# Turning one pair of token tiles on VectorE and through DRAM instead of on TensorE, in a two-layer Fourier mixer with MLPs

## The chip, the cores and the metric

One core of one Trainium2 chip runs the whole program. The metric is the device time of one execution in microseconds (us); the median over the runs is compared. On the core five engines run their own queues in order: TensorE (in the profile PE for matmuls, PEld for weight loads), VectorE (DVE), ScalarE (ACT), GpSimd (POOL) and SyncE (SP), which here issues most DMAs. An engine waits on semaphores for the others, so an instruction that waits holds up all that stands behind it in its queue.

## The reference

`x` is 2048 tokens by 576 features. Two layers each do a Fourier step and an MLP step, both with a layer norm ahead and a residual:

```python
def _A_ref(x, dft_seq_re, dft_seq_im, dft_hid_re, dft_hid_im):
    a = jnp.einsum("bsd,ed->bse", x, dft_hid_re)
    b = jnp.einsum("bsd,ed->bse", x, dft_hid_im)
    return jnp.einsum("ts,bse->bte", dft_seq_re, a) - jnp.einsum("ts,bse->bte", dft_seq_im, b)
def _B_ref(x, w1, b1, w2, b2):
    y = _layernorm(x, axis=-1)
    h = _gelu(jnp.einsum("bsd,df->bsf", y, w1) + b1)
    return jnp.einsum("bsf,fd->bsd", h, w2) + b2
...
    x = x + _A_ref(_layernorm(x, axis=-1), ...)
    x = x + _B_ref(_layernorm(x, axis=-1), ...)
    x = x + _A_ref(_layernorm(x, axis=-1), ...)
    x = x + _B_ref(_layernorm(x, axis=-1), ...)
```

`w1` is 576 by 4608, `w2` is 4608 by 576. All is 32-bit floating point.

## The kernel before, in words

**Arithmetic.** Every large product is done in three TensorE passes over a high and a low part of each operand (`PASSES`): ScalarE copies the high part into a rounded 32-bit type, VectorE (or GpSimd) subtracts it from the value for the low part. Most products also use a scheme with seven block products for a two by two block matrix: sums of blocks are formed first, and the seven results are added up by VectorE, GpSimd and ScalarE.

**Order of the program.** A layer begins with a sequence phase (`Sequence`), which multiplies by the 2048 by 2048 matrices `cs` and writes `uv_mid`. Then, for each half of the tokens, a feature phase (`hidden`) multiplies by the 576-wide matrices, adds the residual and normalizes, and an MLP (`mlp`) follows. So there are two sequence phases, four feature phases and four MLPs. The MLP of a half is a generator that is already advanced while the feature phase ends.

**Sequence phase** (`Sequence.run`). After the first two token blocks it goes through steps, seven per output tile `t` (products in `ORDER`), each 24 matmuls of 128x288 (`mms`). In step `n` the queues get, in this order: loads of `cs` blocks that have found a free place (`load_c`); the low part of step `n + 2` (`low`, VectorE, with up to one more subtraction that forms a sum of blocks in place and then frees a block); once per tile `sums` for the next tile, one addition and one subtraction of 128x1024 on VectorE; the high part of step `n + 3` (`high`, ScalarE); the matmuls; and `post`, which adds the product up. At the end of a tile `turned` transposes it in 32x32 squares on VectorE.

**Pumps.** A generator `weights` prepares the seven block sums of `w1` in the background, one piece in two pumps: high part on ScalarE, low part on VectorE, a sum for a later piece on GpSimd, and a store to `w1_parts`. The store is issued by ScalarE during the first sequence phase, by SyncE later. The sequence phase pumps twice at the end of most steps. In the first MLP the pumps stand at fixed places of a group (`BEHIND`), and the blocks of `w2` are prepared there too (`make`, with `due` places). By the second half all weights come ready from DRAM.

**Feature phase** (`hidden`, half = 8 tiles of 128 tokens, `n` = 0 to 7). Step `n` loads tile `n + 2`, splits the turned input of tile `n + 1` (`turn`: ScalarE high, VectorE low), finishes the norm of tile `n - 1` (ScalarE), and does 54 matmuls (`KH` = 9 parts, 3 passes, 2 halves of features). Then VectorE adds the product to the residual and takes the statistics (`norms`, `stats`; GpSimd does the power). Line 198 is the helper for additions, 201 for subtractions, 211 for all large matmuls, 208 for VectorE's 32x32 transposes, 258 for normalizing.

The MLP needs the normalized tokens with features on partitions. Tiles are turned in pairs: pair `j` is tiles `2j` and `2j + 1` of the order, which give four blocks b12, b22, b11 and b21 (feature half by token half). The three first pairs go like this: `rests` spreads the last 32 features of each block (96 columns, ScalarE), `turn_blocks` transposes on TensorE (eight of 128x128, line 991; four of 128x96, line 994) into PSUM, ScalarE copies out (995, 996), `turn_sums` makes high and low parts of three blocks in two groups and then four sums with VectorE, and `turn_parts` makes the high and low parts of the sums. `turn_blocks` of pairs 0, 1 and 2 stands after the product of `n` = 2, 4 and 6, and `turn_sums` of pairs 0 and 1 inside `n` = 3 and 5.

The last pair goes another way, since nothing is left to hide it: the last tile is normalized by VectorE (line 962), VectorE forms the sums first (t1, t3, t2, t4 in this order; t2 needs t1, t4 needs t2), and `turn_y` transposes all seven blocks on TensorE (14 transposes, line 1035; 7 of the rests, line 1045) in four groups of two blocks, groups in the order `(2, 4, 0, 6)` of the list `blocks`. Each group's high part is copied by ScalarE and its low part subtracted by VectorE (`split`). Matmuls of the MLP for the first half of the tokens (`next(mlp)`) fill TensorE before and between. After them the MLP's products 1, 6, 2, 5, 7, 3, 4 for the second half begin, product `i` with the block at place `RIGHT_T[i]` of `y`.

Of the kernel before, what the change touches and what calls it, by code (L numbers as in the profile page):

```python
# [15 lines left out]
P = 128  # L16
# [26 lines left out]
RIGHT_T = {3: 0, 2: 1, 1: 2, 5: 3, 7: 4, 6: 5, 4: 6}  # L43
# [21 lines left out]
BEHIND = (0, 2, 2, 4, 5, 6, 15, 16, 16, 17, 17, 19, 21, 21)  # L65
H_AT = (8704, 22400)
# [94 lines left out]
def spectral_mixer(ctx: ExitStack, tc: tile.TileContext, x, dh, c0, cs, w1, b1, w2, b2, out):  # L161
# [16 lines left out]
    w1s = nc.dram_tensor("w1_parts", (NQ, 7, P, 5 * P), F32, kind="Internal").ap()  # L178
    w2s = nc.dram_tensor("w2_parts", (NG, 7, P, 2, 2 * DH), F32, kind="Internal").ap()
# [84 lines left out]
    def weights():  # L264
# [44 lines left out]
        high(0)  # L309
        for n in range(7 * NQ):  # L310
            yield
            low(n)
            if n + 1 < 7 * NQ:
                high(n + 1)
            yield
            keep(n)
# [13 lines left out]
    class Sequence:  # L330
# [357 lines left out]
        def sums(self, t):  # L688
            add(nc.vector, self.tmp(NP, P), self.block(t, 2), self.block(t, 3))
            sub(nc.vector, self.block(t, 2), self.block(t, 2), self.block(t, 0))  # L690
# [67 lines left out]
        def run(self, hidden):  # L758
# [12 lines left out]
            for n, (t, i) in enumerate(steps):  # L771
# [3 lines left out]
                if n % 7 == 2 and t + 1 < NT:  # L775
                    self.sums(t + 1)
                self.load_c()
                if n + 3 < len(steps):
                    self.high(*steps[n + 3])
# [13 lines left out]
                if n % 7 != 2 and n > 3 and (t < NT - 1 or n % 7 < 4):  # L793
                    pump()
                    pump()
# [133 lines left out]
    def hidden(h, mlp):  # L929
# [16 lines left out]
        t8 = {}  # L946

        def norms(n):
# [9 lines left out]
            if n < NP - 1:  # L958
                shift(mv)
                normalize(z, tile_x, mv)  # L960
# [11 lines left out]
            yield  # L972

# [10 lines left out]
        def turn_blocks(j):  # L984
# [4 lines left out]
            for n, e in enumerate((2, 0, 1, 3)):  # L989
# [3 lines left out]
            for n, e in enumerate((2, 0, 1, 3)):  # L993
                nc.tensor.transpose(b[:96, 0, n * P:(n + 1) * P], es(7, 96)[:, e], ident)  # L994
# [14 lines left out]
        def turn_sums(j):  # L1009
            x = t8[j](8 * DH)[:, 6 * P:].rearrange("p (b k) -> p b k", b=4)  # L1010
            b11, b12, b22, b21 = (x[:, k] for k in range(4))
            parts(j, slice(2, 4), slice(0, 2))
            parts(j, slice(0, 1), slice(2, 3))
# [10 lines left out]
        def turn_y(j):  # L1024
            v = t8[j](8, DH)
            at = slice(j * P, (j + 1) * P)
            blocks = (1, 3, 2, 4, 5, 6, 7)
# [23 lines left out]
        for n in range(NP):  # L1051
# [6 lines left out]
            if n >= 2 and n % 2 == 0:  # L1058
                rests(n // 2 - 1)
            if n == NP - 3:  # L1060
# [25 lines left out]
            if n in (3, 5):  # L1086
                turn_parts((n - 3) // 2)
            if n >= 2 and n % 2 == 0:
# [32 lines left out]
    def mlp(hid, store, first, ends, before, after):  # L1121
# [3 lines left out]
        stores[0] = nc.sync  # L1125
# [383 lines left out]
```

## Time and profile before

| | |
|---|---|
| median of 3 runs | 2622.78 us (2622.07 to 2624.11) |
| the profiled execution | 2624.75 us |
| its span, first to last instruction | 2623.0 us |
| granted TensorE clock | 1.000 |
| busy: PE, PEld, DVE, ACT, POOL | 2614.4, 2466.3, 1836.8, 1120.2, 791.5 us |
| first sequence phase, its steps | about 79 to 372 us |
| first feature phase and MLP | to about 848 us |
| moved by DMA | 544.91 MB, 208 GB/s over the span |

A group in the profile is a line of the kernel, an engine, an operation and the tiles that it writes and reads, with its count, its busy time, the mean of one in ns, and the idle time of that engine just before, with what ended it. `R` and `A` are the two large areas in SBUF (rounded and plain type), `bank` is PSUM. A wait is put down to the instruction that released it last. The chain is followed back from the last instruction; a piece on it is what the end hung on.

### The profile page before, as it was taken

What the parts mean: (1) busy time and instruction counts of PE and PEld (TensorE: products, weight loads), DVE (VectorE), ACT (ScalarE), POOL (GpSimd) and SP (SyncE); (2) the same over time, 40 slices, a digit from 0 to 9 for tenths busy, and PEclk for the clock granted to TensorE, in tenths of its full rate; (3) what the DMA queues carried; (4) which work ended last, traced back from release to release, by engine and by line L of the source; (5) the groups of instructions that cost most, each with busy time, mean ns of one, the idle gap of its engine ahead of it and who ended that gap; (6) DMA issues with size and microseconds to landing.
All of it is one profiled execution on the core that took longest, in us unless ns stands there. A gap on an engine that the chain in (4) does not pass through costs nothing.

```text
span 2623.0 us, 44794 instructions
## 1 busy us (share of the span) xinstructions
PE 2614.4 (100%) x17252; PEld 2466.3 (94%) x17252; DVE 1836.8 (70%) x2580; ACT 1120.2 (43%) x1821; POOL 791.5 (30%) x638
## 2 busy tenths in 40 slices
PE   9999999999999999999999999999999999999999
PEld 9999999899999989998999999999999999899998
DVE  8999987778787765556687776576555557655555
ACT  7555555555553443333354333353333325433332
POOL 5334333544444332222251000132122233322222
PEclk9999999999999999999999999999999999999999
DMA  6667676778788666676544343756666685666664
GB/s 226 223 236 234 234 255 215 266 278 301 279 299 300 178 202 195 194 222 210 173 175 135 122 124 124 211 159 194 193 195 194 195 268 169 199 195 195 194 194 155
DMA packets 223238, 544.91 MB, mean 208 GB/s; under 512 B 23712, under 2 KB 74912, under 8 KB 222880
## 3 DMA queue, kind: packets, MB, share of 16 engines
q1 hardware_dynamic: 210496, 513.91, 62.2%
q10 hardware_dynamic: 12528, 28.12, 2.8%
q8 instruction: 137, 2.24, 0.3%
q14 instruction: 77, 0.63, 0.1%
HBM read 429.87 MB, written 114.72 MB: 208 GB/s over the span
## 4 chain that ended last, share of the span: by engine, by line
PE 92%; DVE 5%; DMA 1%; issue 1%; POOL 1%; ACT 0%; DVEq 0%; ACTq 0%; SPq 0%; POOLq 0%
PE bank L211 91%; DVE R L201 3%; DVE A L201 1%; DMA w_parts<-R 1%; DMA A<-in_cs 0%; PE bank L991 0%; DVE A L198 0%; PE bank L1035 0%; DVE moments L242 0%; PE bank L994 0%; ACT R L698 0%; DMA A<-in_w 0%; DMA R<-w_parts 0%; PE bank L1045 0%; POOL A L198 0%
## 5 line engine op out<-in xcount | busy, mean ns | idle before, releaser
L211 PE MATMUL bank<-R 128*128 128x288 f32 (+2 forms) x16972 | 2585.9, 314 | 3.9 <-DVE R L201 1.2
L211 PEld LDWEIGHTS bank<-R 128*128 128x128 f32 x16972 | 2434.8, 189 | 150.8 <-DVE R L201 4.3
L198 DVE TENSOR_TENSOR A<-bank,A 128x576 f32<-128x576 f32 (+3 forms) x812 | 567.6, 707 | 510.2 <-PE bank L211 457.7
L201 POOL TENSOR_TENSOR R<-A,R 128x512 fp32r<-128x512 f32 (+1 forms) x292 | 380.0, 1310 | 912.4 <-ACT R L1299 560.6
L201 DVE TENSOR_TENSOR R<-A,R 128x1024 fp32r<-128x1024 f32 (+10 forms) x534 | 535.0, 1028 | 34.6 <-ACT R L698 14.3
L1299 ACT ACTIVATE R<-A 128x512 fp32r<-128x512 f32 x288 | 177.5, 630 | 356.4 <-DVE A L201 219.5
L198 POOL TENSOR_TENSOR A<-A 128x576 f32<-128x576 f32 (+2 forms) x102 | 155.0, 1527 | 531.1 <-ACT A L743 338.9
L1234 ACT ACTIVATE bank<-bank,b1t 128x512 f32<-128x512 f32 (+1 forms) x224 | 144.9, 647 | 350.5 <-DVE bank L198 233.6
L698 ACT ACTIVATE R<-A 128x1024 fp32r<-128x1024 f32 x196 | 205.6, 1054 | 123.8 <-PE bank L211 61.0
L198 DVE TENSOR_TENSOR bank<-bank,A 128x512 f32<-128x512 f32 (+1 forms) x228 | 152.3, 670 | 147.7 <-PE bank L211 147.0
L201 POOL TENSOR_TENSOR A<-A 128x288 f32<-128x288 f32 (+3 forms) x152 | 190.3, 1255 | 198.1 <-DVE R L201 103.6
L201 DVE TENSOR_TENSOR A<-A 128x1024 f32<-128x1024 f32 (+3 forms) x166 | 163.5, 989 | 6.2
L201 DVE TENSOR_TENSOR R<-bank,R 128x512 fp32r<-128x512 f32 x232 | 156.1, 676 | 5.5 <-ACT R L1299 5.0
L1299 ACT ACTIVATE R<-bank 128x512 fp32r<-128x512 f32 x216 | 121.0, 595 | 33.9 <-PE bank L211 33.9
L201 DVE TENSOR_TENSOR A<-bank,A 128x512 f32<-128x512 f32 x144 | 98.1, 681 | 0.4
L1261 ACT ACTIVATE A<-bank 128x512 f32<-128x512 f32 (+1 forms) x76 | 43.7, 575 | 120.2 <-PE bank L211 120.1
L284 ACT ACTIVATE R<-A 128x256 fp32r<-128x256 f32 x126 | 51.9, 412 | 63.7 <-DMA w_parts<-R 27.1
L1234 ACT ACTIVATE A<-bank,b1t 128x512 f32<-128x512 f32 (+1 forms) x76 | 50.5, 665 | 63.4 <-DVE bank L198 63.4
L232 POOL TENSOR_TENSOR moments<-moments,power 128x1 f32<-128x1 f32 x32 | 25.5, 797 | 134.9 <-DVE moments L234 117.5
L285 ACT ACTIVATE R<-A,power,middle 128x128 fp32r<-128x128 f32 x126 | 60.6, 481 | 0.0
L258 ACT ACTIVATE A<-A,moments 128x576 f32<-128x576 f32 x58 | 49.3, 867 | 23.7 <-DMA A<-x_mid 11.7
L198 DVE TENSOR_TENSOR A<-A 128x1024 f32<-128x1024 f32 x28 | 35.8, 1277 | 20.0 <-DMA A<-in_cs 12.3
(70 smaller groups left out, 612.9 us busy)
## 6 DMA issues: line engine op xcount, KB each, us to landing
R<-w_parts SPq DMA_DIRECT2D x504, 320.0 KB, 3.4
R<-w_parts SPq DMA_DIRECT2D x189, 576.0 KB, 3.7
A<-in_cs SPq DMA_DIRECT2D x112, 512.0 KB, 4.5
w_parts<-R SPq DMA_DIRECT2D x63, 576.0 KB, 6.2
w_parts<-R ACTq DMA_DIRECT2D x75, 320.0 KB, 4.3
w_parts<-R SPq DMA_DIRECT2D x51, 320.0 KB, 4.9
uv_mid<-A SPq DMA_DIRECT2D x28, 576.0 KB, 5.4
A<-in_w SPq DMA_DIRECT2D x72, 192.0 KB, 5.4
```

The lines of the kernel that those rows point to most:

```text
L198: engine.tensor_tensor(dst, a, b, op=op)
L201: engine.tensor_tensor(dst, a, b, op=OP.subtract)
L211: nc.tensor.matmul(o, a, b, start=start, stop=stop, skip_group_check=True)
L232: nc.gpsimd.tensor_tensor(mv[:, 3:4], mv[:, 2:3], power[:, 0:1], op=OP.pow)
L258: nc.scalar.activation(dst, src, AF.Identity, bias=mv[:, 4:5], scale=mv[:, 3:4])
L284: nc.scalar.activation(t[:, 1:4:2], src[:, 0:3:2], AF.Copy)
L285: nc.scalar.activation(t[:, 2], src[:, 1], AF.Identity, bias=power[:, 2:3], scale=middle)
L698: nc.scalar.activation(self.cells[t, i](2, NP, P)[:, 0], self.source(t, i), AF.Copy)
L1234: nc.scalar.activation(dst, src, AF.Gelu_apprx_tanh, bias=bias(f))
L1261: nc.scalar.activation(up, o, AF.Copy)
L1299: nc.scalar.activation(H[q, k](2, TC)[:, 0], src, AF.Copy)
```

## The change

Several things are changed at once.

1. In the three feature phases after the first (`flip`, true where the matrices come ready), pair 0 is no longer turned on TensorE. ScalarE normalizes its two tiles into squares of 32 features (`mixed`); VectorE transposes the first tile's two blocks 32 by 32 (`turn_early`, in `n` = 1); in `n` = 2 it forms the four sums and transposes five blocks (`turn_late`). The squares are written to a DRAM tensor `y_mid` (`write_first`, SyncE, three DMAs for each of two parts) and read back in the order that the MLP needs (`read_first`, four DMAs each). `first_parts` then makes the high parts (three ScalarE copies) and low parts (three VectorE subtractions), in `n` = 3 for the first two blocks and in `n` = 4 for the other five, ahead of that tile's addition. `rests`, `turn_blocks`, `turn_sums` and `turn_parts` of pair 0 are gone there.
2. The seven blocks of `y` get another order, in all four phases (`RIGHT_T`, `turn_blocks`, `turn_sums`, `turn_y`), so that the two blocks and the five lie side by side. `turn_sums` makes the parts of its three blocks in one group. In `turn_y` the order of groups stays `(2, 4, 0, 6)`, with another list of blocks.
3. In the sequence phase `sums` is done in two pieces, the addition at place 3 of a tile and the subtraction at place 4, not both at 2. Of the two pumps of a step one goes ahead of `high` of step `n + 3`; the step without pumps is the last of a tile. In `weights` the store of a piece comes one pump later, with the next high part.
4. In the first MLP's group 0 three more steps of `make(0)` are done, and group 1 has two pumps fewer (`BEHIND_1`).

The diff, cut to its core:

```diff
-RIGHT_T = {3: 0, 2: 1, 1: 2, 5: 3, 7: 4, 6: 5, 4: 6}
+RIGHT_T = {2: 0, 1: 1, 3: 2, 4: 3, 5: 4, 6: 5, 7: 6}
+FIRST_AT = ((4224, 0), (10464, 11232))
+BEHIND_1 = (0, 2, 2, 4, 15, 16, 16, 17, 17, 19, 21, 21)
...
-        high(0)
+        done = 0
         for n in range(7 * NQ):
+            if n:
+                keep(n - 1)
+            if done == n:
+                high(n)
+                done += 1
             yield
             low(n)
-            if n + 1 < 7 * NQ:
+            if len(stores) > 1 and n + 1 < 7 * NQ:
                 high(n + 1)
+                done += 1
             yield
-            keep(n)
+        keep(7 * NQ - 1)
...
-                if n % 7 == 2 and t + 1 < NT:
-                    self.sums(t + 1)
+                if n % 7 in (3, 4) and t + 1 < NT:
+                    self.sums(t + 1, (n % 7 - 3,))
                 self.load_c()
+                step = n % 7 != 6 and n > 3 and (t < NT - 1 or n % 7 < 5)
+                if step:
+                    pump()
                 if n + 3 < len(steps):
                     self.high(*steps[n + 3])
...
-                if n % 7 != 2 and n > 3 and (t < NT - 1 or n % 7 < 4):
-                    pump()
+                if step:
                     pump()
...
-                normalize(z, tile_x, mv)
+                if flip and n < 2:
+                    xg = tile_x.rearrange("p e (g i) -> p e g i", i=32)
+                    for e, k in enumerate((0, 3) if n else (2, 1)):
+                        normalize(mixed()[:, k], xg[:, e], mv)
+                else:
+                    normalize(z, tile_x, mv)
...
+        def mixed():
+            return t8[0](8 * DH).rearrange("p (g e i) -> p g e i", e=8, i=32)
+        def wide(k, n):
+            return t8[0](9, 8 * 32)[:, :, 32 * k:32 * (k + n)]
+        def write_first(k, v):
+            for f in range(2):
+                dma(y_mid[k][:, :, f], v[:, 4 * f:4 * f + 4])
+            dma(y_mid[k][:, :, 2], v[:, 8:9].to_broadcast([P, 4, v.shape[2]]))
+        def read_first(k):
+            n = (2, 5)[k] * 32
+            first_x[k] = b = (A if half else R).place(FIRST_AT[half][k], 12 * n)
+            x, src = b(4, 3 * n), y_mid[k].rearrange("(q d) c f x -> c d q (f x)", q=4)
+            for c in range(4):
+                to = x[32 * c:32 * c + 32]
+                dma(to if half else to.bitcast(F32), src[c])
+        def turn_early():
+            nc.vector.transpose(wide(6, 2), wide(1, 2))
+            write_first(0, wide(6, 2))
+        def turn_late():
+            b12, b21, b11, b22, t4, t1, t2, t3 = (mixed()[:, k] for k in range(8))
+            sub(nc.vector, t1, b12, b11)
+            sub(nc.vector, t2, b22, t1)
+            sub(nc.vector, t4, b21, t2)
+            sub(nc.vector, t3, b22, b12)
+            nc.vector.transpose(wide(3, 5), wide(3, 5))
+        def first_parts(k):
+            at, i, n = slice(0, P), (slice(0, 2), slice(2, 7))[k], (2, 5)[k]
+            b = first_x.pop(k)
+            x = b(12 * n * 32)
+            x = (x if half else x.bitcast(F32)).rearrange("p (q f i t) -> p f i q t", q=4, i=n, t=32)
+            for f in range(3):
+                nc.scalar.activation(y[:, i, f, at].rearrange("p i (q t) -> p i q t", q=4), x[:, f], AF.Copy)
+            for f in (2, 0, 1):
+                part = slice(64, 96) if f == 2 else slice(0, P)
+                hi, to = (y[part, i, m, at].rearrange("p i (q t) -> p i q t", q=4) for m in (f, 2 if f == 2 else 3 + f))
+                sub(nc.vector, to, x[part, f], hi.bitcast(F32))
+            b.free()
...
-            parts(j, slice(2, 4), slice(0, 2))
-            parts(j, slice(0, 1), slice(2, 3))
+            parts(j, slice(0, 3), slice(0, 3))
...
-            blocks = (1, 3, 2, 4, 5, 6, 7)
+            blocks = (3, 2, 1, 7, 4, 6, 5)
             for m, i0 in enumerate((2, 4, 0, 6)):
...
-            if n >= 2 and n % 2 == 0:
+            if flip and n == 1:
+                turn_early()
+            if flip and n == 2:
+                read_first(0)
+                turn_late()
+            elif n >= 2 and n % 2 == 0:
                 rests(n // 2 - 1)
+            if flip and n == 3:
+                write_first(1, wide(3, 5))
+                read_first(1)
+                t8s.give(t8.pop(0))
...
-                if n in (3, 5) and k == 2:
+                if n in (3, 5) and k == 2 and (n == 5 or not flip):
                     turn_sums((n - 3) // 2)
                 if k == 4:
                     next(ln, None)
+                if flip and n in (3, 4) and k == 6:
+                    first_parts(n - 3)
...
-            if n in (3, 5):
+            if n == 5 or n == 3 and not flip:
                 turn_parts((n - 3) // 2)
-            if n >= 2 and n % 2 == 0:
+            if flip and n == 2:
+                h.ring += 2
+            elif n >= 2 and n % 2 == 0:
                 turn_blocks(n // 2 - 1)
...
-            for _ in range(BEHIND.count(at[0]) if to is None and group[0] else 0):
+            for _ in range((BEHIND if group[0] > 1 else BEHIND_1).count(at[0]) if to is None and group[0] else 0):
...
-                due.extend((n, step) for n, (_, step) in zip((3, 4), soon))
+                due.extend((n, step) for n, (_, step) in zip((3, 4, 8, 11, 12), soon + late[:3]))
+                late = [(0, late[3][1]), *late[4:]]
```

More of the change, by code (lines that the diff above doesn't have):

```diff
@@ L178, in spectral_mixer @@
     w1s = nc.dram_tensor("w1_parts", (NQ, 7, P, 5 * P), F32, kind="Internal").ap()
+    y_mid = [nc.dram_tensor(f"y_mid{k}", (P, 4, 3, n * 32), F32, kind="Internal").ap() for k, n in enumerate((2, 5))]
     w2s = nc.dram_tensor("w2_parts", (NG, 7, P, 2, 2 * DH), F32, kind="Internal").ap()
@@ L686, in block, with sums @@
             return self.live[t, k](NP, P)
-        def sums(self, t):
-            add(nc.vector, self.tmp(NP, P), self.block(t, 2), self.block(t, 3))
-            sub(nc.vector, self.block(t, 2), self.block(t, 2), self.block(t, 0))
+        def sums(self, t, which=(0, 1)):
+            if 0 in which:
+                add(nc.vector, self.tmp(NP, P), self.block(t, 2), self.block(t, 3))
+            if 1 in which:
+                sub(nc.vector, self.block(t, 2), self.block(t, 2), self.block(t, 0))
         def source(self, t, i):
@@ L945, in hidden @@
         dma(b2t(D), b2.to_broadcast([P, D]))
-        t8 = {}
+        t8, flip, first_x = {}, h.made, {}
         def norms(n):
@@ L972, in norms @@
             yield
+        def mixed():
+            return t8[0](8 * DH).rearrange("p (g e i) -> p e g i", e=8, i=32)
+        def wide(k, n):
[33 more added lines that the diff above has]
+            b.free()
         def rests(j):
@@ L988, in turn_blocks @@
             a, b = space(), space()
-            for n, e in enumerate((2, 0, 1, 3)):
+            for n, e in enumerate((3, 2, 1, 0)):
                 for k in range(2):
@@ L992, in turn_blocks @@
                                         v[:, e, k * P:(k + 1) * P], ident)
-            for n, e in enumerate((2, 0, 1, 3)):
+            for n, e in enumerate((3, 2, 1, 0)):
                 nc.tensor.transpose(b[:96, 0, n * P:(n + 1) * P], es(7, 96)[:, e], ident)
@@ L1010, in turn_sums @@
             x = t8[j](8 * DH)[:, 6 * P:].rearrange("p (b k) -> p b k", b=4)
-            b11, b12, b22, b21 = (x[:, k] for k in range(4))
-            parts(j, slice(2, 4), slice(0, 2))
-            parts(j, slice(0, 1), slice(2, 3))
+            b21, b11, b22, b12 = (x[:, k] for k in range(4))
+            parts(j, slice(0, 3), slice(0, 3))
             g = nc.vector
@@ L1124, in mlp @@
         half, X, Y = hid.half, hid.X, hid.Y
-        stores[0] = nc.sync
+        stores[:] = nc.sync, nc.sync
         xv, y = X(2, NP, DH), Y(7, 5, TC)
@@ L1382, in mlp @@
         for g in range(NG + 1):
-            at[0], group[0] = 0, g or not first
+            at[0], group[0] = 0, g if first else NG
             if first and not g:
                 soon, late = make(0)
-                due.extend((n, step) for n, (_, step) in zip((3, 4), soon))
+                due.extend((n, step) for n, (_, step) in zip((3, 4, 8, 11, 12), soon + late[:3]))
+                late = [(0, late[3][1]), *late[4:]]
             elif first:
```

## The prediction

> **What bounds the kernel now.** I read the page first, then the chain, then the waits of the weight loads, whole and by stretch, then the timeline at the places that the diff touches.
>
> ```profile
> span 2623.0 us, 44794 instructions
> PE 2614.4 (100%) x17252; PEld 2466.3 (94%) x17252; DVE 1836.8 (70%) x2580; ACT 1120.2 (43%) x1821; POOL 791.5 (30%) x638
> PE 92%; DVE 5%; DMA 1%; issue 1%; POOL 1%; ACT 0%; DVEq 0%; ACTq 0%; SPq 0%; POOLq 0%
> ```
>
> TensorE (PE) is the bound: it is busy for the whole span and carries 92% of the chain. So only two things can make the kernel faster, TensorE work taken away or TensorE waits taken away, and each new wait counts in full. The ends of matmuls are modelled, so I read the waits from the weight loads (columns: us in total, times, longest):
>
> ```profile
> PEld bank L211 <- DVE R L201: 4.3, 10, 0.9
> PEld bank L211 <- DVE bank L198: 1.9, 3, 1.0
> PEld bank L211 <- DVE A L198: 1.4, 5, 0.6
> ...
> PEld bank L1035 <- DVE A L201: 0.7, 4, 0.2
> ```
>
> These rows are 8.3 us of waits in the whole program, so little is left to win this way. Nearly all of them lie in two places, the first sequence phase and the first groups of the first MLP. The same view for 143 to 343 us:
>
> ```profile
> PEld bank L211 <- DVE R L201: 3.3, 8, 0.9
> PEld bank L211 <- ACT A L733: 0.4, 1, 0.4
> ```
>
> and for 443 to 502 us:
>
> ```profile
> PEld bank L211 <- POOL R L201: 1.0, 1, 1.0
> PEld bank L211 <- DVE bank L198: 1.0, 1, 1.0
> PEld bank L211 <- DVE R L201: 0.8, 1, 0.8
> PEld bank L211 <- DVE A L198: 0.6, 1, 0.6
> ```
>
> So 3.7 us can be won in the first stretch and 3.4 us in the second. About 0.2% (5.2 us) is what a measurement of this kernel can tell from no change.
>
> **Part 1, sums and pumps in the sequence phase.** The first row is the table by stretches (after the stretch and its length: PE, PEld, DVE, ACT, POOL busy), the second the page's group of the additions that `sums` does.
>
> ```profile
> 143.00:343.00 200.00, 198.32 (x1478) 196.00 (x1477) 189.58 (x186) 112.91 (x204) 72.62 (x49) 1.00 0.68 230
> L198 DVE TENSOR_TENSOR A<-A 128x1024 f32<-128x1024 f32 x28 | 35.8, 1277 | 20.0 <-DMA A<-in_cs 12.3 <-DVE R L201 4.4 <-issue 3.2
> ```
>
> VectorE (DVE) is busy 189.6 of 200 us here, and those 28 additions stood idle before them for 20 us, 12.3 of these until a block of `cs` had landed. VectorE is late, so it frees the block late, so the load is issued late, so the addition waits: a closed loop that costs TensorE 3.7 us. The change puts the addition one step of 24 matmuls later, and the subtraction two steps later. A step is 24 x 0.133 = 3.2 us (14.38 us for 108 matmuls, a row below), more than a usual wait of this group (20.0 / 28 = 0.7 us). Work is the same (one more weight piece in the phase, and no pump in the step that ends with the turn). On ScalarE (ACT) the weight store and its high parts now come ahead of `high(n + 3)`; the store waits for a VectorE subtraction that has had a step to finish. I take the whole 3.7 us as gone; bounds 0 and 4.
>
> **Part 2, the first MLP.** Two pumps fewer in group 1 (`BEHIND_1`), and three of four steps of `make(0)` done in group 0, where TensorE does not wait. That relieves VectorE where two waits stand (1.0 and 0.6 us). The third wait, 1.0 us on GpSimd (POOL), had a weight subtraction in front of it on the chain:
>
> ```profile
> 478.48 0.97 POOL A L201
> ```
>
> Its pump is one of the two taken out, but GpSimd's other pieces there stay dense. The fourth, 0.8 us, is untouched. I take 1.5 us as won; bounds 0 and 3.4.
>
> **Part 3, transposes taken away.** Chain, start and length, around the turn of pair one in the second half of layer 0; then the group of these transposes:
>
> ```profile
> 870.49 0.87 PE bank L991 x8
> 871.36 0.44 PE bank L994 x4
> 871.80 14.38 PE bank L211 x108
> ...
> 901.88 0.87 PE bank L991 x8
> ...
> L991 PE MATMUL bank<-ident,A 128*128 128x128 f32 x96 | 12.4, 273 | 0.0
> ```
>
> Twelve transposes take 0.87 + 0.44 = 1.31 us of TensorE; three phases, 3 x 1.31 = 3.9 us less. One instruction has 273 ns, but eight are done in 0.87 us, 109 ns apart. The Trainium skill, page "TensorE: Matmul & The Clock Gate", Part 4, gives about 275 ns for one in a kernel; by that figure 36 transposes would be an estimated 9.9 us, but the spacing decides here, and the trace has it at 109 ns.
>
> **Part 4, what replaces them.** VectorE's own transposes (576 and 1440 elements) by the row of 1152 below: 0.69 and 1.72 us, hidden, as TensorE never waits for them. What matters is `first_parts`: its three ScalarE copies and three VectorE subtractions stand in tiles 3 and 4 ahead of the addition of that tile's product, and so ahead of that tile's norm.
>
> ```profile
> L208 DVE STREAM_TRANSPOSE A<-A 128x1152 f32<-128x1152 f32 x32 | 44.1, 1377 | 2.9
> L1169 ACT ACTIVATE R<-A 128x576 fp32r<-128x576 f32 x63 | 42.2, 676 | 17.1 <-PE bank L211 7.4 <-DVE A L201 7.1 <-POOL A L201 2.6
> L201 DVE TENSOR_TENSOR R<-A,R 128x576 fp32r<-128x576 f32 x63 | 53.4, 847 | 0.1
> L201 DVE TENSOR_TENSOR R<-A,R 32x512 fp32r<-32x512 f32 x8 | 5.6, 699 | 0.2
> L977 ACT ACTIVATE A<-A 128x384 f32<-128x384 f32 x12 | 6.3, 526 | 0.4
> ```
>
> The timeline of the second half of layer 0: additions of tiles 4 and 5, and the normalizing of tile 5.
>
> ```profile
> 886.22 0.76 DVE L198 TENSOR_TENSOR A<-bank,A 128x576 f32<-128x576 f32 x1
> ...
> 896.48 0.75 DVE L198 TENSOR_TENSOR A<-bank,A 128x576 f32<-128x576 f32 x1
> ...
> 900.22 0.87 ACT L258 ACTIVATE A<-A,moments 128x576 f32<-128x576 f32 x1
> ```
>
> Before the change tile 4 is added at 886.22, as its product ends; tile 5 is normalized at 900.22 + 0.87 = 901.09; TensorE comes to transpose tiles 4 and 5 at 901.88. The slack is 0.8 us. From addition to normalized takes 901.09 - 896.48 = 4.6 us. After: count from the end of tile 3's product. Its addition waits some 0.8 us for `first_parts(0)` (its three subtractions, by the same rows, 0.7 + 0.4 + 0.4 = 1.5 us, are the most); 4.6 us to normalized; 0.53 for `rests(1)`; three copies of 640 elements, 0.75 each, 2.2; then subtractions of 32x640 and two of 128x640, about 0.7 + 0.9 + 0.9 = 2.5, as the first of them needs the last copy. 0.8 + 4.6 + 0.5 + 2.2 + 2.5 = 10.6 us, and tile 4's product takes 54 x 0.133 = 7.2. So tile 4 is added 3.4 us late, all that follows is as late, and with 0.8 us of slack and 0.4 saved in `turn_sums(1)` (one 32-row subtraction fewer, 0.7, behind a longer copy), TensorE waits 2.2 us at the transposes of pair three. Three phases: 6.6 us. Bounds: with tile 3 not delayed, copies of 0.68 and subtractions of 0.7 each, 9.2 us and a wait of 0.8 a phase; with 1.5, 2.2 and 3 x 0.94, 11.6 us and a wait of 3.2. If tile 3's norm comes sooner than I count there is none, so the lowest end is 0.
>
> SyncE gets 6 writes and 8 reads a phase. `read_first` waits on SyncE for its writes; behind it stand the loads of the next tiles, which have a tile's time, 7.2 us. The trip through DRAM is not in this trace; nearest rows, us from issue to landing:
>
> ```profile
> uv_mid<-A SPq DMA_DIRECT2D x28, 576.0 KB, 5.4
> ...
> R<-uv_mid SPq DMA_DIRECT2D x64, 144.0 KB, 4.0
> ```
>
> VectorE's second turn ends 4.6 + 1.7 + 1.7 = 8.0 us after the end of tile 1's product (normalized, four subtractions by the row of 441.36 below, 1440 elements turned), 0.8 us into tile 3. Write and read, 5.4 + 4.0, end 10.2 us into tile 3. The copies can start 7.2 + 0.8 + 4.6 + 0.5 = 13.1 us into it. It fits by 3 us, less what seven issues on one queue take.
>
> **Part 5, blocks reordered in `turn_y`.** All four phases. The groups are still taken in the order 2, 4, 0, 6, but the first group now holds b22 and t4, and t4 is the last of the four VectorE subtractions. Timeline of the first phase:
>
> ```profile
> 441.36 1.69 DVE L201 TENSOR_TENSOR A<-A 128x288 f32<-128x288 f32 x4
> 441.70 0.74 PEld L1035 LDWEIGHTS bank<-ident,A 128*128 128x128 f32 x6
> ...
> 442.61 0.85 PEld L1035 LDWEIGHTS bank<-ident,A 128*128 128x128 f32 x8 [0.17 <-DVE A L201]
> ...
> 443.43 1.74 PEld L211 LDWEIGHTS bank<-R 128*128 128x128 f32 x14
> 443.44 1.82 ACT L204 ACTIVATE R<-bank 128x512 fp32r<-128x512 f32 x4
> ...
> 444.05 1.29 DVE L201 TENSOR_TENSOR R<-bank,R 128x512 fp32r<-128x512 f32 x2
> ...
> 445.26 1.47 DVE L201 TENSOR_TENSOR R<-A,R 128x1024 fp32r<-128x1024 f32 x1
> ...
> 445.87 1.26 PEld L211 LDWEIGHTS bank<-R 128*128 128x128 f32 x10
> ...
> 446.65 0.68 DVE L201 TENSOR_TENSOR R<-bank,R 128x512 fp32r<-128x512 f32 x1
> ```
>
> Today b11 goes first and t1, t3, t2, t4 follow as VectorE makes them. After: two transposes, then a wait for t4 (441.36 + 1.69 = 443.05, seen about 443.1), then twelve, 12 x 0.109 = 1.3: ready at 444.4 instead of 443.43, 1.0 us late. Second, product 1 of the next half used block group one and will use group three, whose low part is the row at 446.65, ending 447.33, and about 0.2 later as its first copy waits for t4's transposes. TensorE would be there at 445.87 + 1.0 plus one matmul (0.12), 447.0, and waits until 447.5: 0.5 us more. 1.45 us a phase, 5.8 us in four; bounds 1.0 and 1.7, so 4.0 and 6.8. What hides it: nothing, as TensorE is not idle anywhere behind it.
>
> **The sum.** -3.7 - 1.5 - 3.9 + 6.6 + 5.8 = +3.3 us. The profiled execution took 2624.75 us (1.75 around its span), so 2628.05; the median shown, 2622.78, lies 1.97 lower, and gives 2626.1 us.
>
> **Rivals.**
> - *No wait at pair three.* If tile 4 is added in time, parts 3 and 4 give -3.9 alone: 2622.78 - 3.3 = 2619.5. For it: VectorE is also relieved of pair one's old sums. Against: these lay in tiles 2 and 3, and the chain from tile 4 on is as long as before.
> - *Both reorderings cost nothing,* the t4 wait too: -9.1, 2613.7. Against: the order of the subtractions is plain in the trace, and the 0.7 us of waits there are already theirs.
> - *The DRAM trip lands late, slower.* Place: `first_parts(1)`. From 3 us later than counted, each us delays tile 4's addition and with it tile 6's product and pair three by one more, in three phases; 6 us late, 3 over, give +9, 2635. For it: the writes are in runs of 256 and 640 bytes, and SyncE issues all of them in order behind the loads of tiles 3 to 5. The Trainium skill, page "DMA: Bandwidth & Descriptors", Specifications, asks for 512 bytes or more, below which an engine reads, modifies and writes; that would slow the first, small write; no row here shows it.
> - *A transpose counts its own duration.* 36 x 0.273 = 9.8 instead of 3.9, by the group row: 2620.2. Against: the chain's 0.87 for eight. The Trainium skill's 275 ns, taken as a cost, is this rival.
>
> **How the numbers follow.** Forecast as summed, 0.54. With every bound at its low end (0.8 us a phase at pair three) it would be 2617.9, at its high end 2635.3; as they hardly meet, I give it 2620 to 2632. No wait at pair three 0.21; both free 0.06; late DRAM 0.12; own duration 0.03; something unseen 0.04. Faster by over 0.2%: "both free", a fifth of "no wait" and little else, 0.12. Slower by over 0.2% (over 2628.0): late DRAM 0.12 and the upper third of the forecast 0.19, with a part of the unseen, 0.32. Within: 0.56. The range, 2617.5 to 2632.5, holds the forecast, most of "no wait" and part of the late trip.
>
> **What would show it.** Right: no waits of weight loads between 143 and 343 us; 72 transposes on the line that is L991 today, instead of 96, with the chain's 0.87 gone at the first of three turns; a new wait of some 2 us before the second turn left in those phases, released by ScalarE's normalizing; a wait of 1.0 us at `turn_y` after its second transpose in all four phases, released by VectorE. Wrong: no such gap, or gaps before a tile's product released by a DMA of the new tensor, or waits left in the sequence phase.

## The result, and the profile after

The changed kernel takes 2643.57 us (median of 6 runs, 2642.48 to 2645.26), the kernel before, run beside it, 2623.27 us (6 runs): a ratio of 1.0072, with a 95% interval of 1.0061 to 1.0082. It is 20.3 us slower, where 2626.1 us and a range up to 2632.5 had been forecast. The profiled executions are 20.5 us apart (spans of 2643.5 and 2623.0 us).

The page's head for the kernel after:

```profile
span 2643.5 us, 44772 instructions
PE 2616.9 (99%) x17216; PEld 2468.1 (93%) x17216; DVE 1832.5 (69%) x2568; ACT 1116.9 (42%) x1818; POOL 785.9 (30%) x638
```

36 matmuls fewer, as planned, and TensorE is no longer busy for the whole span. Helper lines have moved by three (additions 201, subtractions 204, the copies of `split` 207, large matmuls 214, normalizing 261); the turn of a pair on TensorE is now lines 1053 and 1056, that of `turn_y` line 1096, and the copies of `first_parts` are line 1029. The waits of the weight loads (us in total, times, longest):

```profile
PEld bank L1053 <- ACT A L261: 14.7, 5, 4.5
PEld bank L214 <- DVE R L204: 5.6, 11, 1.1
PEld bank L1096 <- DVE A L204: 4.4, 4, 1.2
```

The first row is the wait that part 4 of the prediction foresaw, at the transposes of a pair for ScalarE's normalizing, but more than twice as large. The third is `turn_y`'s wait for the last subtraction. The table by stretches around pair three in the second half of layer 0 shows something that no part had (length; busy PE, PEld, DVE, ACT, POOL; then the granted clock, the DMA share and GB/s):

```profile
900.00:905.00 5.00, 0.78 (x8) 0.55 (x6) 4.78 (x10) 3.86 (x5) 1.06 (x2) 0.85 0.35 118
905.00:910.00 5.00, 5.00 (x22) 4.96 (x23) 3.68 (x9) 4.23 (x6) 2.49 (x2) 0.50 0.00 0
910.00:915.00 5.00, 5.00 (x39) 5.00 (x38) 3.75 (x5) 0.05 (x1) 1.57 (x1) 0.96 0.34 98
...
1745.00:1750.00 5.00, 5.00 (x23) 4.96 (x22) 3.68 (x9) 3.98 (x6) 2.37 (x3) 0.50 0.00 0
...
2221.00:2226.00 5.00, 5.00 (x27) 4.96 (x28) 3.72 (x9) 4.27 (x6) 2.51 (x2) 0.66 0.00 0
```

Behind the wait TensorE looks fully busy, and yet only 22 matmuls begin in 5 us instead of 39: the granted clock is 0.50. The loss is 5 x 0.50, 5 x 0.50 and 5 x 0.34 us in the three phases, and 5 x 0.04 us in the next row of the first: some 6.9 us, a second price of the same wait. In windows of 1 us the clock stands at 0.50 for 6.8, 6.8 and 3.4 us, in part still within the wait.

The timeline of that phase shows where the 4.5 us come from. TensorE ends tile 1's product at 861.4; a product is 7.2 us, so tile 2's ends at 868.6, tile 3's at 875.8 and tile 4's at 883.0. (Picked rows; others between them are left out.)

```profile
861.43 0.76 DVE L201 TENSOR_TENSOR A<-bank,A 128x576 f32<-128x576 f32 x1 [0.86 <-PE bank L214]
864.25 1.17 ACT L207 ACTIVATE R<-R 128x1152 fp32r<-128x1152 f32 x1 [4.55 <-DMA R<-uv_mid]
865.72 1.15 ACT L261 ACTIVATE A<-A,moments 128x288 f32<-128x288 f32 x2
866.72 2.92 DVE L204 TENSOR_TENSOR A<-A 128x288 f32<-128x288 f32 x4
867.01 1.46 POOL L201 TENSOR_TENSOR A<-A 128x576 f32<-128x576 f32 x1 [2.90 <-ACT A L261]
869.68 1.68 DVE L1021 STREAM_TRANSPOSE A<-A 128x1440 f32<-128x1440 f32 x1
871.28 0.72 DVE L201 TENSOR_TENSOR A<-bank,A 128x576 f32<-128x576 f32 x1
871.42 2.97 SPq L198 DMA_DIRECT2D y_mid<-A  x3
...
877.38 1.61 DVE L204 TENSOR_TENSOR R<-A,R 32x256 fp32r<-32x256 f32 x3 [2.68 <-ACT R L1029]
878.79 1.73 SPq L198 DMA_DIRECT2D A<-y_mid  x4
878.90 0.75 DVE L201 TENSOR_TENSOR A<-bank,A 128x576 f32<-128x576 f32 x1
883.22 0.87 ACT L261 ACTIVATE A<-A,moments 128x576 f32<-128x576 f32 x1
885.46 2.00 ACT L1029 ACTIVATE R<-A 128x640 fp32r<-128x640 f32 x3 [0.82 <-DMA A<-y_mid]
887.49 2.39 DVE L204 TENSOR_TENSOR R<-A,R 32x640 fp32r<-32x640 f32 x3 [5.13 <-ACT R L1029]
889.80 0.75 DVE L201 TENSOR_TENSOR A<-bank,A 128x576 f32<-128x576 f32 x1
...
900.29 0.75 DVE L201 TENSOR_TENSOR A<-bank,A 128x576 f32<-128x576 f32 x1
904.03 0.87 ACT L261 ACTIVATE A<-A,moments 128x576 f32<-128x576 f32 x1
904.95 0.71 PEld L1053 LDWEIGHTS bank<-ident,A 128*128 128x128 f32 x4 [4.45 <-ACT A L261]
```

Read the additions on line 201. Tile 2's comes 2.7 us after its product's end, because the four subtractions and the second turn stand ahead of it. Tile 3's comes 3.1 us late behind the first two blocks' subtractions; its norm ends at 884.1, after TensorE has come to pair two, which waits 0.9 us. Tile 4's is 6.8 us late. The five blocks' copies begin only at 885.46. Tile 3's norm and `rests` hold ScalarE until 884.6, and then the data were still on the way for 0.8 us, as SyncE had stood for its own write before it could issue the read (waits of its queue, 850 to 900 us; then ScalarE's waits for `y_mid` in the whole run, total and count):

```profile
SPq L198 <- DMA y_mid<-A: 4.8, 2, 4.3
...
  ACT R L1029: 1.1, 2
```

The copies of the five blocks waited for their data 0.8, 0 and 0.3 us in the three phases, so the trip through DRAM is a small part of the delay. In the other two phases tile 4's addition is 5.8 and 5.4 us late.

In the first of these phases tile 5's addition follows 10.5 us later, as before the change (10.3), and so pair three waits.

In the first sequence phase the additions of `sums` no longer wait: 20.0 us of idle time before them have become 1.4 (the group by form):

```profile
L201 DVE TENSOR_TENSOR A<-A 128x1024 f32<-128x1024 f32 x28 | 34.1, 1218 | 1.4 <-DMA A<-in_cs 1.4
```

But TensorE has not gained. The waits of its weight loads from 100 to 400 us are 3.7 us as before, with a new one released by ScalarE among them:

```profile
PEld bank L214 <- DVE R L204: 2.2, 3, 1.1
PEld bank L214 <- ACT A L752: 1.5, 1, 1.5
```

Its timeline shows where ScalarE stood: the high part of a weight piece (line 287) waited for GpSimd's sum, and that for its load. SyncE had issued the load at 112.5, after standing 9.2 us for a VectorE subtraction ahead of a load of `cs`. The copy that frees the bank (line 752, at 121.57) is behind it on ScalarE.

```profile
117.85 2.03 POOL L201 TENSOR_TENSOR A<-A 128x384 f32<-128x384 f32 x1 [14.74 <-DMA A<-in_w]
119.91 0.42 ACT L287 ACTIVATE R<-A 128x256 fp32r<-128x256 f32 x1 [3.01 <-POOL A L201]
```

In the first MLP there is less waiting. From 442 to 501 us, where 3.4 us stood, the longer one of the second row (0.7) and the third row (0.3) are left; the others belong to the last turn:

```profile
PEld bank L1096 <- DVE A L204: 1.2, 1, 1.2
PEld bank L214 <- DVE R L204: 1.1, 2, 0.7
PEld bank L214 <- DVE bank L201: 0.3, 1, 0.3
```

The last turn in the first phase looks as part 5 had it, two transposes and then the wait:

```profile
440.76 0.24 PEld L1096 LDWEIGHTS bank<-ident,A 128*128 128x128 f32 x2
442.22 1.29 PEld L1096 LDWEIGHTS bank<-ident,A 128*128 128x128 f32 x12 [1.22 <-DVE A L204]
...
446.49 1.61 PEld L214 LDWEIGHTS bank<-R 128*128 128x128 f32 x13 [0.38 <-DVE R L204]
```

### The profile page after: what moved, and what is told of

The parts are those of the page before. It is cut to its first block, busy times and chain, and to the rows that moved or that the text cites. A ratio compares the mean times of both kernels' runs of the same rounds, so it can differ in the third digit from the quotient of the medians.

```text
span 2643.5 us, 44772 instructions
## 1 busy us (share of the span) xinstructions
PE 2616.9 (99%) x17216; PEld 2468.1 (93%) x17216; DVE 1832.5 (69%) x2568; ACT 1116.9 (42%) x1818; POOL 785.9 (30%) x638
## 5 line engine op out<-in xcount | busy, mean ns | idle before, releaser
L204 DVE TENSOR_TENSOR R<-A,R 128x1024 fp32r<-128x1024 f32 (+8 forms) x510 | 521.4, 1045 | 75.1 <-ACT R L709 29.9
L201 POOL TENSOR_TENSOR A<-A 128x576 f32<-128x576 f32 (+2 forms) x102 | 146.0, 1437 | 540.3 <-ACT A L754 341.1
L709 ACT ACTIVATE R<-A 128x1024 fp32r<-128x1024 f32 x196 | 204.3, 1053 | 109.4 <-PE bank L214 61.6
L204 POOL TENSOR_TENSOR A<-A 128x288 f32<-128x288 f32 (+3 forms) x152 | 184.8, 1219 | 192.2 <-DVE R L204 105.0
L235 POOL TENSOR_TENSOR moments<-moments,power 128x1 f32<-128x1 f32 x32 | 36.0, 1126 | 150.5 <-DVE moments L237 128.0
L261 ACT ACTIVATE A<-A,moments 128x576 f32<-128x576 f32 (+1 forms) x64 | 51.0, 820 | 22.8 <-DMA A<-x_mid 10.8
L1243 ACT ACTIVATE R<-A 128x576 fp32r<-128x576 f32 x63 | 42.2, 676 | 16.6 <-DVE A L204 7.1
```

Source lines behind the costliest of these rows:

```text
L201: engine.tensor_tensor(dst, a, b, op=op)
L204: engine.tensor_tensor(dst, a, b, op=OP.subtract)
L235: nc.gpsimd.tensor_tensor(mv[:, 3:4], mv[:, 2:3], power[:, 0:1], op=OP.pow)
L261: nc.scalar.activation(dst, src, AF.Identity, bias=mv[:, 4:5], scale=mv[:, 3:4])
L709: nc.scalar.activation(self.cells[t, i](2, NP, P)[:, 0], self.source(t, i), AF.Copy)
L1243: nc.scalar.activation(got2[g, i](2, 2, DH)[:, :, 0], src, AF.Copy)
```

## The experiments

**e1, without the turn by VectorE.** `t8, flip, first_x = {}, False, {}`.

> The changed kernel with flip set to False: pair one is turned by TensorE again in all four feature phases, everything else of the change stays. Theory A (the loss lies in what the turn by VectorE puts in front of the additions of tiles 2, 3 and 4): the three phases lose their waits of 14.8 us and the 7.0 us of matmuls at a low granted clock behind them, and pay 3.9 us for 36 transposes again, so 2643.6 - 17.9 = 2625.7 us, with no wait over 0.5 us at the transposes of pairs two and three. Rival B (the reordered blocks of pairs two and three make these waits): they stay, and the time is 2643.6 + 3.9 = 2647.5 us.

2627.15 us beside 2625.20 for the kernel before, run with it (ratio 1.0009, 1.0000 to 1.0018), and no wait at all on line 1053. So the three phases with the turn cost 20.3 - 1.9 = 18.4 us net (expected 17.9), and the reordered blocks have no part in pairs two and three.

**e4, TensorE kept busy in the wait.** In `turn_blocks`, behind the first tile's transposes:

```diff
+                if flip and j == 2 and n == 1:
+                    for _ in range(40):
+                        nc.tensor.transpose(b[:, 1, :P], ident, ident)
```

> The changed kernel with 40 transposes of a constant into an unused half bank, between tile 4's and tile 5's transposes of pair three in the three phases: TensorE works through the 4.4 us in which it waited. Nothing of the output depends on them. Theory A (the wait itself brings the granted clock down, and the matmuls behind it run at half speed): tile 5's transposes start when they did, the granted clock stays at 1.0 behind them, and some 7.0 us go, 2636.6 us. Rival E (the clock goes down for another reason, such as the time since the start of the phase): the clock is 0.5 behind the wait as before, and the time is 2643 us or, with the transposes taking longer than the wait, 2645.

2639.00 us beside 2625.20: 13.8 us slower than before instead of 20.3, so 6.5 us come back. Windows of this run:

```profile
900.00:905.00 5.00, 5.00 (x47) 5.00 (x46) 4.68 (x11) 3.49 (x4) 1.04 (x1) 1.00 0.41 118
905.00:910.00 5.00, 5.00 (x41) 4.76 (x40) 4.13 (x9) 4.64 (x7) 2.53 (x2) 1.00 0.01 3
```

The clock stays at 1.00, and 41 matmuls begin where 22 did. Tile 5's transposes still come at 905.4. So the idle time itself brings the clock down, and a wait of 4.5 us costs up to 7: its length and 2.5 us of matmuls at half speed.

**e2, the same work in another order.**

```diff
                 read_first(0)
-                turn_late()
...
-                if flip and n in (3, 4) and k == 6:
-                    first_parts(n - 3)
...
+            if flip and n in (3, 5):
+                first_parts(n // 4)
             if flip and n == 2:
+                turn_late()
                 h.ring += 2
```

> The changed kernel with the same instructions in the three phases, but in another order: the second turn of VectorE stands behind the addition and moments of tile 2, the parts of the first two blocks behind those of tile 3, and the parts of the five others behind those of tile 5, no longer ahead of an addition. Theory A (the order on VectorE and ScalarE): the waits at pairs two and three and the low clock behind them go, 2643.6 - 21.8 = 2621.8 us; with some 1 us left in a phase 2625. Rival C (the trip through DRAM and its 14 issues on SyncE, which delay the loads of the later tiles): waits before tiles or pairs stay at 2 us or more in each phase, released by DMA or by what follows a DMA, and the time is 2635 us or more.

2642.08 us beside 2625.20 (ratio 1.0067, 1.0054 to 1.0079): hardly better. Theory A alone falls. It holds for the first part of the chain: all additions up to tile 4's come on time, and pair two waits no more. But pair three still waits 3.4 us in this phase (3.6 and 2.4 in the other two). Its timeline, ScalarE and then SyncE:

```profile
888.76 1.17 ACT L207 ACTIVATE R<-R 128x1152 fp32r<-128x1152 f32 x1 [3.41 <-DMA R<-uv_mid]
...
890.24 0.87 ACT L261 ACTIVATE A<-A,moments 128x576 f32<-128x576 f32 x1
```

```profile
869.20 0.60 SPq L198 DMA_DIRECT2D A<-in_x  x1
874.17 1.95 SPq L198 DMA_DIRECT2D y_mid<-A  x3
879.02 1.73 SPq L198 DMA_DIRECT2D A<-y_mid  x4
881.16 1.73 SPq L198 DMA_DIRECT2D R<-uv_mid  x4
```

SyncE stands from 869.8 to 874.2 for the turn, and from 876.1 to 879.0 for its own writes; the loads of a later tile's source, behind them, are issued at 881.2. ScalarE's copy of that source waits until 888.76, and tile 4's norm, behind it on ScalarE, ends at 891.1 (886.8 in e9, below). Rival C's queue is a second cause, and the write is followed by more waits than its own read.

**e12, the five blocks alone moved.** Everything of the change as it is, but `read_first(1)` behind the loads of step 4 and `first_parts(1)` behind tile 6's addition:

```diff
                 write_first(1, wide(3, 5))
-                read_first(1)
                 t8s.give(t8.pop(0))
+            if flip and n == 4:
+                read_first(1)
...
-                if flip and n in (3, 4) and k == 6:
-                    first_parts(n - 3)
+                if flip and n == 3 and k == 6:
+                    first_parts(0)
...
+            if flip and n == 6:
+                first_parts(1)
```

> The changed kernel with two moves alone: the read of the five other blocks behind the loads of the next tile, and their parts behind tile 6's addition. The second turn and the first two blocks' parts stay ahead of the additions of tiles 2 and 3. Theory (the five blocks' parts ahead of tile 4's addition, and what their read holds up, are the cause of the waits at pair three; the others only of the 0.9 us at pair two): 2643.6 - 13.3 - 7.0 = 2623.3 us, with up to 1 us left at pair two in each phase, 2626. Rival (the second turn, which makes tile 2's addition 2.8 us late, is the cause, and the delay goes on to tile 5 by itself): waits of 2 us or more stay at pair three, over 2633 us.

2629.72 us beside 2624.75 (ratio 1.0020, 1.0011 to 1.0029). The waits at pair three are gone, and the clock behind them is 1.00; 0.9 us or less at pair two stay in each phase, as the theory has it. It is 5.0 us slower than before, where up to 2.7 had been expected, as the last turn's waits for VectorE grew from 4.4 to 7.8 us: tiles 6 and 7 are late now. At the last turn of the first of these phases the clock was also at 0.50 for 3.4 us, some 1.7 us more. So the five blocks' parts ahead of tile 4's addition, with the read that holds up SyncE, are what pair three's waits hang on: with them moved, the second turn and the two blocks' parts leave only pair two's. No run moves the read alone or the parts alone, so their shares are not told apart; in the changed kernel itself the copies waited for the read only 1.1 us in all, which speaks for the parts.

**e9, both moves.** The order of e2, the read as in e12, the five parts in tile 6's product (ahead of its addition), and the last turn's groups as `(0, 4, 6, 2)`. Against e2:

```diff
-                read_first(1)
                 t8s.give(t8.pop(0))
+            if flip and n == 4:
+                read_first(1)
...
+                if flip and n == 6 and k == 6:
+                    first_parts(1)
...
-            if flip and n in (3, 5):
-                first_parts(n // 4)
+            if flip and n == 3:
+                first_parts(0)
```

> The order of e2_order with two more moves and the order of e3_turn_y: the read of the five other blocks is issued behind the loads of the next tile instead of ahead of them, so that SyncE waits for the write only with nothing due behind it, and these blocks' parts are made in tile 6's product instead of ahead of tile 5's norm. Theory A+C (in e2_order the load of tile 6's source lands at 888.7 us because SyncE stood waiting for the second turn and its writes, and ScalarE holds tile 4's norm behind that source): the waits at pair three go, and with those of the last turn 2643.6 - 21.8 - 5.8 = 2616.0 us; with 1 us left in a phase 2619. Rival F (ScalarE and VectorE have too much to do in tiles 4 and 5 whatever the order): the waits at pair three stay at 2 to 3.5 us, and the time is that of e2_order less the last turn's 5.8, 2636.3 us.

2627.07 us beside 2624.31 (ratio 1.0010, 1.0001 to 1.0019). No wait is left on line 1053, and the clock is 1.00 around pairs two and three in all three phases: rival F falls. But the time is 2.8 us over the kernel before, where 4 to 7 less had been expected. 7.6 us of waits stand at the last turn; in the timeline:

```profile
899.13 2.39 DVE L204 TENSOR_TENSOR R<-A,R 32x640 fp32r<-32x640 f32 x3 [1.70 <-ACT R L1029]
901.43 0.75 DVE L201 TENSOR_TENSOR A<-bank,A 128x576 f32<-128x576 f32 x1
...
908.63 0.75 DVE L201 TENSOR_TENSOR A<-bank,A 128x576 f32<-128x576 f32 x1
```

Tile 6's product ends at 897.6, and its addition waits for the five parts until 901.4; tile 7's is 2.6 us late in turn, and the last turn with it. The work's harm has only moved on to the next place without slack. In the third phase the two waits there, 1.9 and 0.5 us, also brought the clock down to 0.50 for 3.4 us, some 1.7 us more:

```profile
2215.00:2220.00 5.00, 3.74 (x18) 3.51 (x19) 4.70 (x10) 2.46 (x6) 2.52 (x4) 0.66 0.00 0
```

**e3, the last turn's order alone.**

```diff
-            for m, i0 in enumerate((2, 4, 0, 6)):
+            for m, i0 in enumerate((0, 4, 6, 2)):
```

> The changed kernel with the groups of the last turn taken in the order 0, 4, 6, 2 instead of 2, 4, 0, 6, so that the block subtracted last is transposed last, and product 1's block first. Theory A (the first group waits for the last subtraction, and product 1 of the next stage for the third group's low part): the waits of 1.0 to 1.1 us at the second transpose and of 0.4 us before product 1 go in all four phases, 4 x 1.45 = 5.8 us, so 2637.8 us. Rival D (the last turn waits for something else, such as normalized tiles or banks): the wait moves to another transpose and keeps its size, 2643 us.

2638.80 us beside 2625.20, 13.6 slower than before instead of 20.3. That is 6.7 us back, with 5.8 expected; the runs scatter by some us, and the waits tell more exactly: line 1096 waits 0.3 us in all instead of 4.4, and product 1's waits are gone.

```profile
PEld bank L1096 <- DVE A L204: 0.3, 1, 0.3
```

**e5, e7 and e6, three parts by themselves, in the kernel before.** First the moved sums (`n % 7 in (3, 4)`, `self.sums(t + 1, (n % 7 - 3,))`):

> The kernel before with one part of the change: the addition of the sums one step later and the subtraction two steps later in the sequence phase. Theory G (the prediction's: the addition waits for its block's load, and moved later it waits no more): TensorE's 3.7 us of waits between 143 and 343 us go, 3.7 us less than before. Rival H (VectorE has no time left in this phase, so that the wait goes over to the next subtraction, at 154 and 310 us, as in the changed kernel): waits of 1.0 and 0.5 us released by VectorE stay at these two places, and the gain is 1 to 2 us.

2621.80 us beside 2624.31 (ratio 0.9992, 0.9983 to 1.0000). Between 100 and 400 us no wait is left: theory G, all of its 3.7 us of waits. Rival H falls, as nothing stays at 154 and 310 us. Then the order of the weight pieces and their pumps (`keep(n - 1)` and `high(n)` at the start of a piece, one of the two pumps ahead of `high(*steps[n + 3])`):

> The kernel before with one part of the change: the order in which a weight piece is stored, loaded anew, copied and subtracted in the sequence phase, and where its two pumps stand in a step. Theory J (this part makes the new wait at 120 us: the weight load stands on SyncE behind a wait for a sequence block, so that ScalarE's copy of the piece waits, and behind it the copy that frees TensorE's bank): a wait of 1.0 to 1.5 us released by ScalarE near 120 us, and 1 to 2 us more than before. Rival K (the moved sums make it): no wait near 120 us, and the waits between 143 and 343 us as before, no change.

2626.04 us beside 2624.31 (ratio 1.0007, 0.9998 to 1.0016); the place was wrong, and that ScalarE releases the waits right. From 100 to 400 us:

```profile
PEld bank L211 <- ACT A L747: 5.0, 5, 2.5
```

All waits for VectorE have gone there and 5.0 us for ScalarE stand in their place. The longest, in the timeline of this run:

```profile
346.87 0.36 ACTq L299 DMA_DIRECT2D w_parts<-R  x1
347.34 0.42 ACT L284 ACTIVATE R<-A 128x256 fp32r<-128x256 f32 x1 [4.10 <-DVE R L201]
...
348.99 0.39 ACT L747 ACTIVATE A<-bank 128x288 f32<-128x288 f32 x1
...
349.43 1.73 PEld L211 LDWEIGHTS bank<-R 128*128 128x128 f32 x8 [2.49 <-ACT A L747]
```

The piece's store is issued by ScalarE, now right behind the subtraction that makes its data, and VectorE is late; ScalarE stands 4.1 us for it, and the copy on line 747 that frees TensorE's bank stands behind. So the store is what holds ScalarE here, not the weight load of theory J; that load is behind the changed kernel's wait at 122 us, shown above. Behind the wait of 2.5 us the granted clock was 0.50 from 349.7 to 353.1 us in the profiled execution. And the first MLP (`BEHIND_1`, five steps of `make(0)` in group 0):

> The kernel before with one part of the change: fewer pumps in group 1 of the first MLP and three steps of the second stage's weights made in group 0. Theory (from the two traces): the waits of 0.3, 0.7 and 1.0 us at 471, 473 and 480 us go and a wait of some 0.5 us stays near 499, so 2.4 us less than before. The prediction had 1.5, with 0 and 3.4 as bounds. Rival: the gain needs the sequence phase's pieces to come earlier as well, and at least one of the three waits stays.

2621.67 us beside 2624.31 (ratio 0.9989, 0.9980 to 0.9997), 2.6 us less; the waits from 443 to 502 us go from 3.4 to 1.3. These terms are about as large as what a run can tell, so the waits carry the verdicts and the times only agree.

**e11 and e10, what the runs favour.** The sums and the MLP alone:

> The kernel before with the moved sums and the changed first MLP alone: no turn by VectorE, old blocks, old order of the weight pieces. Theory (the two parts add up): 3.7 + 2.6 = 6.3 us less than before. Rival (both draw on the same free time of VectorE, as later pumps move from one to the other): 3 to 4 us less.

2618.82 us beside 2624.75 (ratio 0.9979, 0.9970 to 0.9988), 5.9 us less than before. And all parts in their better form, e9 with the weight pieces in the old order and

```diff
-                if flip and n == 6 and k == 6:
-                    first_parts(1)
...
-            if flip and n == 3:
-                first_parts(0)
+            if flip and n in (3, 6):
+                first_parts(n // 6)
```

> All parts of the change in the form that the runs so far favour: the order of e9_read_late, but with the five blocks' parts behind tile 6's addition and moments instead of ahead of it; the last turn's groups in the order 0, 4, 6, 2; the moved sums, but the weight pieces in their old order; the first MLP as changed. Theory (the waits of 1.8 and 0.5 us at the last turn in e9_read_late come from that addition, 3.8 us late): they go, and what is left against the kernel before is -3.7 (sequence phase), -2.4 to -3.4 (first MLP) and -3.9 (36 transposes), 10 to 11 us less than before. Rival (VectorE is short of time in tiles 6 and 7 wherever the parts stand): waits of 1 us or more stay at the last turn of the three phases, and the gain is 4 to 7 us.

2618.27 us beside 2624.75 (ratio 0.9976, 0.9967 to 0.9985), 6.5 us less, below the 10 to 11 expected and inside the rival's 4 to 7. The last turn still waits for VectorE's subtractions, 0.8 us at the longest:

```profile
PEld bank L1088 <- DVE A L204: 4.4, 7, 0.8
```

These were 0.7 us before the change, so 3.7 us more. Against the two parts alone (e11), the turn by VectorE with the new order of blocks gains 0.6 us, less than the runs can tell: the 3.9 us of transposes are nearly eaten up there. Both versions beat both kernels.

## Why the prediction was wrong, by its own steps

**The sum.** Measured in the profiled executions, term by term: sequence phase 0 (forecast -3.7), first MLP -2.4 (-1.5), transposes -3.9 (-3.9), pairs two and three +15.2 of waits (14.7 on line 1053 and 0.5 before a product) and +6.9 of low clock (+6.6 for both), last turn +5.2 (+5.8). That is +21.0, against 20.5 between the spans. The transposes are their count times the spacing of before; the rest is read from waits and clock.

**Part 4 failed most, and in its size.** Place and releaser were right, also what stands ahead of what. The step "Its addition waits some 0.8 us for `first_parts(0)`" counted the delay of tile 3 at 0.8 us; it was 3.1 (2.2 at the least, in the third phase). Its cause lies a tile earlier: "VectorE's second turn ends ... 0.8 us into tile 3" was 2.7, because tile 1's norm took 5.4 us from its addition (a copy waiting for its load stands ahead of it on ScalarE) where a norm of 4.6 us had been taken from another tile, and because four subtractions took 2.9 us where 1.7 had been taken from a quieter place.

From the end of tile 3's product to tile 4's addition it was 3.1 + 5.2 (norm) + 0.5 (`rests`) + 0.8 (wait for the data) + 2.0 (copies) + 2.4 (subtractions) = 14.0 us, where 10.6 had been counted. So tile 4 was added 6.8 us late, not 3.4, and 2.3 us of the difference are tile 3's delay. The steps lie in a row on one chain without slack, so each adds to the next.

"It fits by 3 us" was wrong as well: the trip took 14 us (871.4 to 885.4), not 9.4, as the writes take 3.0 us and the reads 1.7 us to issue, and SyncE waits 4.3 us in between. But the chain ahead of the copies was late itself, so they waited for the data 0.8 us here and 1.1 us in all three phases. The late trip, put down as a rival with 0.12, was there and took little part.

**Missing altogether: the clock.** Every us of TensorE's wait was counted once. In e4 the wait without idle time gave 6.5 us back. The Trainium skill, page "TensorE: Matmul & The Clock Gate", Part 1, says that about 3.4 us of idle time bring the clock to half and that as much busy time brings it back. The runs agree on the length: every stretch at 0.50 before the program's end lasted 3.4 us or twice that. They do not bear out 3.4 us of idle time as what it takes: the clock also fell behind a wait of 2.5 us in e7 and behind 1.9 and 0.5 us in the third phase of e9, and did not behind 2.4 and 1.8 us in the third phase of e2. So the forecast wait of 2.2 us, at most 3.2, could have cost more than its length too; what decides it for waits of this size stays open.

**Part 1: one half right, one wrong.** The moved sums do what was forecast. The step that failed is "the store waits for a VectorE subtraction that has had a step to finish": with VectorE busy for 189.6 of 200 us, a step was not enough. Between 100 and 400 us ScalarE stood 55.2 us for VectorE's subtractions ahead of the high parts, 18.3 before the change; in e7 it was 73.3 us, and 5.0 us of TensorE's waits came of it. It was costed at nothing, and no cover had been named for the bank copies behind it. In the changed kernel the one such wait, 1.5 us, came by the late weight load instead. The 2.2 us of waits for VectorE, at 155, 311 and 383 us, stand neither in e5 nor in e7; what makes them is open.

**Parts 2, 3 and 5 held.** -2.4 lies within the bounds of part 2; 72 transposes are left on what is now line 1053; the last turn's waits of 1.0 to 1.2 and 0.4 us a phase are 5.9 us, 0.7 of which stood there before: 5.2 us more, where 5.8 had been forecast.

**The rivals.** "No wait at pair three" and "both free" are refuted by the wait; "late trip" by the 1.1 us that the copies waited for their data; "own duration" by e10 against e11: 0.6 us less with 3.7 us more of waits makes 4.3 us for the 36 transposes, not 9.8.

## What to carry to other kernels

When work is put ahead of a step on a chain without slack, follow its delay through every later step of that chain, not only to the first wait, with durations from the very tiles concerned, for each engine queue and for the DMA queue. An instruction that only issues a DMA still held up its engine until its data were there (ScalarE 4.1 us in e7): a store right behind the step that makes its data, on an engine whose other work frees TensorE's banks, is a wait in the making. And a long wait of TensorE can cost more than its length: here all of 3.4 us and more did, and some of 2 to 2.5 us, alone or two together.

## What the runs showed of the hardware

- TensorE's granted clock fell to 0.50 during or right behind each of the eight waits of 3.4 us or more (three in the changed kernel, two in e2, three in e3), for 3.4 or 6.8 us. Of eight places with a wait or two close waits of 2.2 to 4.2 us in all, each wait 2.5 at most, it fell for 3.4 us at three (e7, 2.5 us; the third phase of e9, 1.9 and 0.5; the first of e12, 0.7 and 1.5) and stayed at 1.00 at five (the third phase of e2, 2.4 and 1.8; the others of e9 and e12). So the length of a wait alone does not decide it.
- In e4 forty transposes of a constant in place of the wait kept the clock at 1.00 in all three phases. The Trainium skill, page "TensorE: Matmul & The Clock Gate", Part 4, says that transposes do not count as work of TensorE in the same way; in this run they did.
- Four VectorE subtractions of 128x288 took 2.92 us with a GpSimd addition of 1.46 us beside them (rows at 866.72 and 867.01; 2.98 and 2.91 us in the other two phases), and 1.86 us in e2, where GpSimd's addition came after them. The Trainium skill, page "SBUF — State Buffer", section "SBUF: two separate sides", tells of a port pair that VectorE and GpSimd hold in turn; the rows agree, but no run here tried it by itself.
